# Layer 1 of a two-layer fp32 MLP: the third token tile's first products as seven block products, and another order of work at the layer boundary

## The chip, the cores and the metric

The kernel runs on one core of a Trainium2 chip. The metric is the device time of one execution in microseconds (us). The core has a matrix engine (PE, with its weight loads shown apart as PEld), a vector engine (DVE), an activation engine (ACT), a general engine (POOL) and a queue engine (SP) that issues the transfers; each takes its own instructions in order, and semaphores let one wait for another.

## The reference, cut to what matters

```python
# attention with a decay gives x: 1536 tokens x 512
h = x @ w_in;   g = h * tanh(softplus(h));   x = g @ w_out      # layer 1, d_ff = 2048
h = x @ w_in2;  g = h * sigmoid(h);          out = g @ w_out2   # layer 2
```

## The kernel before, in words

**Splitting.** A fp32 product is made of three products of a shorter type: each matrix is held as a high part (a cast, ACT) and a low part (what the cast lost, DVE or POOL), and a product is high x high, low x high and high x low, all added up in PSUM. A weight comes from memory as 512 KB by one transfer into a staging slot; ACT (L140, L141) and DVE (L172, L176) unpack it, ACT casts it (L240) and POOL makes its low part (L241). High and low parts live in places of an "arena" that are handed out by `take` and returned by `give`.

**Tiling.** There are three token tiles of 512 tokens (0, 1, 2), and the 2048 columns of a layer are taken in steps `p` of two slices of 128. Steps 0 to 7 are layer 1, steps 8 to 15 layer 2. The text below says "step 4" for p = 4.

**Seven instead of eight.** For tiles 0 and 1 together, the eight block products (two tiles, two halves of the inner dimension, two slices) are made as seven, by a scheme that multiplies sums of blocks: `m1, m5, m6, m2, m7, m3, m4`. Each is six matmuls of 128x512, so 42 for what would take 48. It needs sums of the token blocks (`sums`, made once per layer) and of the weight blocks (`T` for the first matrix, `S` for the second, `sum_pair`, on POOL). The same scheme serves the second products, `s1, s5, s6, s2, s7, s3, s4`. Tile 2 has no partner: its first products are `h0` and `h1` (12 matmuls of 128x512 each, L1160), its second ones `o0` and `o1` (12 each, L1215). From step 4 on, all of PSUM is eight banks Z0 to Z7 of 512 columns.

**What sets the order.** Nothing is scheduled by the compiler: the order on each engine is the order in which Python issues the instructions. For steps 4 to 15 (class `Step`) it is written out as a string per step in `plans`: visits parted by `;`, each a list of names. `m..`, `s..`, `h`, `o` are products with what follows them; `a0/a1` the activation of `h`, `l0/l1` its low part; `ts`, `n4` sums of activated blocks into the pad `F`; `q0/q1` their high and low parts; `p` begins unpacking a weight (ACT; a digit names the bank used as scratch), `d` is one unpacking or weight-summing operation (DVE or POOL), `w` puts one weight part into the arena. `into` adds a finished block into the layer's accumulators. At the end of each visit `pump` issues a transfer if a staging slot is free. Steps 2 and 3 (class `Block`, `m..` in the list `core`) and the second products of slices 4 to 7 (`emit_o`, list `os`) come just before step 4.

**Staging.** There are four slots: two of their own (`slot`) and two halves of `slab`. From step 8 on `slab` is an accumulator, so the last steps load through two slots only.

**The boundary.** Layer 2 needs all of layer 1's output: step 7 ends with the last additions, then the output is split again into high and low parts (`c00` ... `c11` for tiles 0 and 1, `x2` for tile 2), and the sums of blocks for layer 2 are made from it (`s_1`, `s_4`, `s_3`, then `hi`/`low`). Step 8 therefore uses eight plain products (`e0` to `e3`) in place of the seven; step 9 is the first that needs the sums.

Of the kernel before, what the change touches and what calls it, by code (L numbers as in the profile page):

```python
# [17 lines left out]
def decay_attention_mish_silu_kernel(  # L18
# [39 lines left out]
    slab = const.tile([P, 2048], F32, name="slab")  # L58
# [93 lines left out]
    made = {}  # L152
    adder = [nc.vector]
# [68 lines left out]
    def run_parts(k=None):  # L222
        for _ in range(len(parts) if k is None else min(k, len(parts))):
# [3 lines left out]
            homes_of[key] = take(True), take(True)  # L227
            hi, lo = [t.rearrange("p (k c) -> p k c", k=2) if len(key) > 2 else t for t in homes_of[key]]
            wtiles[key] = hi, lo
# [6 lines left out]
            else:  # L236
                uses_left[key] = 2
# [361 lines left out]
    def emit_o(t, n, first, last):  # L599
# [4 lines left out]
        if first:  # L604
            po[t] = [(ps_o, late[-1])[j // 2].tile([P, T], F32, tag="o", name="po") for j in range(4)]
# [83 lines left out]
    def make_sums(pool, other):  # L689
# [22 lines left out]
            [low(3, fx)],  # L712
        ])
# [166 lines left out]
    for i, (t, f) in enumerate(steps):  # L880
        n = i + PH
        if n == N:
# [7 lines left out]
            pads.append(late[0].tile([P, 4, T], F32, name="F"))  # L890
            eye = late[0].tile([P, P], F32, name="eye")
# [113 lines left out]
    for item in items:  # L1005
# [40 lines left out]
    class Step:  # L1046

        def __init__(self, p):
            self.p, self.mm = p, 2 * p // NF
            self.opens = p == NF // 2  # L1050
# [3 lines left out]
            self.Z = Z if self.mm == 0 else Z[6:] + Z[:6]  # L1054
            self.quad = [self.Z[2 * i : 2 * i + 2] for i in range(4)]

        def product(self, dst, xq, wq, start):
# [51 lines left out]
        def m4(self):  # L1109
            p = self.p  # L1110
            self.product(6, (1, 1), 3, False)
            for key in ((2 * p, 0), (2 * p + 1, 0), (p, "T", 0), (p, "T", 1)):
                read(key)
            self.split("21", self.Z[6])
# [31 lines left out]
        def part(self, k, low):  # L1146
# [5 lines left out]
            low.tensor_tensor(out=lo, in0=f, in1=hi.bitcast(F32), op=sub)  # L1152

# [42 lines left out]
        def q1(self):  # L1196
            self.part(1, nc.vector if self.late or self.opens else nc.gpsimd)
# [24 lines left out]
        def seed(self):  # L1222
            self.seeded = True
            self.po = [self.Z[i] for i in (2, 3, 6, 7)]
            for k in range(4):
                nc.scalar.copy(self.po[k], accs[self.mm, 2][:, k])

        def o0(self):
            if not self.po:
                self.po = [self.Z[i] for i in ((2, 3, 6, 7) if self.late else (0, 1, 4, 3) if self.opens else range(4))]  # L1230
# [59 lines left out]
        def s7(self):  # L1290
            self.second(0, 2, 1, False)
            self.into(0, 2, 0)
            if self.opens:
                accs[1, 1] = homes[0].tile([P, 4, T], F32, tag="acc", name="acc")
            self.into(1, 0, 3, True)

        def s3(self):
            self.second(2, 3, "22", False)
            self.into(0, 0, 2)
# [19 lines left out]
    def x2():  # L1319
        for k in range(4):  # L1320
            hi, lo = [x[:, k] for x in x_tile(2)]
            z = Z[(2, 3, 6, 7)[k]]
# [7 lines left out]
    def c(t, k, e):  # L1330
        cast_x(t, k)(e)

    def s_1():
        g = [F[:, 2:4], F[:, 0:2]]
        tt(out=g[0], in0=a1[:, 0:2], in1=a1[:, 2:4], op=add)
        lows[0] = cast(sums[0], g[0])
        tt(out=g[1], in0=g[0], in1=a0[:, 0:2], op=sub)
        lows[1] = cast(sums[1], g[1])
# [21 lines left out]
    def close(st):  # L1360
# [13 lines left out]
    extras = {"x2": x2, "s_1": s_1, "s_3": s_3, "s_4": s_4, "hi2": lambda: hi(2), "hi3": lambda: hi(3)}  # L1374
    extras |= {f"low{i}": lambda i=i: low(i) for i in range(4)}
    extras |= {f"c{t}{k}": lambda t=t, k=k: c(t, k, nc.gpsimd if k > t else nc.vector) for t in range(2) for k in range(2)}
    extras |= {"p": lambda: run_pre(1, 0), **{f"p{i}": lambda i=i: run_pre(1, 0, st.Z[i]) for i in (4, 5, 6, 7)}, "d": lambda: run_split(1, 0), "w": lambda: run_parts(1)}
    tail = "m7 d d; m3; m4 ts; h0 a0 q0 n4 w; l0 p6 h1 a1 q1 p4 w; d l1 d o0 d d; o1 w w d d; s1 d d; s5 w; s6; s2 w; s7; s3; s4 p4"
    steady = "m1 p5 d d; m5; m6 d d w w; m2 d d; " + tail
    plans = {  # L1380
        GF: "m1 p4 p5; m5; m6 d d d d; m2 w w d d; " + tail,
        NF // 2 - 1: "m1 p5 d d d d; m5; m6 w w; m2; m7; m3 ts; m4 n4 q0; h0 a0 l0; h1 a1 l1 q1; "
        "s1; s5 table w; s6 p w; s2; s7 c01 seed; s3 c00; s4 c11 c10; o0 s_1; o1",
        NF // 2: "e0 low0 low1 x2 d d; e1 s_4 p w; e2 s_3 d d; e3; h0 a0 w l0 d d d d ts; h1 a1 p l1 n4 q0 w q1 w d d; o0; o1 ; s1 p w; s5 d d; s6 d d d d w; s2; s7 hi2 w hi3 w; s3 low2; s4 p4",
        NF // 2 + 1: steady.replace("m6", "m6 low3"),
# [65 lines left out]
```

## Time and profile before

| | us |
|---|---|
| median of 3 runs | 551.08 (550.48 to 551.21) |
| the profiled execution | 551.02 |
| its span in the trace | 549.1 |
| PE busy | 539.3 (98%) |
| DVE / ACT / POOL busy | 404.0 / 338.2 / 288.3 |
| granted PE clock, mean | 0.999 |

The time is what the device took for the whole execution; the span runs from the first profiled instruction to the last, and 1.92 us of the time lie outside it. Matmuls are pipelined: a row shows 0.39 us for one of 128x512, though the next starts sooner. So the time that PE loses is read from starts: so many matmuls between two starts, at the spacing that a stretch without waits shows.

### The profile page before, as it was taken

Reading aid. Unit: us, or ns where it says so; the run is one execution under the profiler, and the core shown is the slowest. Engines: PE = TensorE matmul, PEld = TensorE weight load, DVE = VectorE, ACT = ScalarE, POOL = GpSimd, SP = SyncE. Lnnn points to the kernel's source line nnn. Section 1 sums busy time; section 2 is a strip of 40 time slices with the busy share of each in tenths; the row PEclk is TensorE's granted clock in tenths of the full one; section 3 lists DMA queues with packets and bytes.
Section 4 is the critical chain, followed back from the end, with each engine's and each line's share of the span. In section 5 each row is a group of like instructions: output and inputs, shape, how many; then the busy total and the mean of one; then the engine's idle time right before and its main releaser. Section 6 shows DMA issues by size and latency. Waiting matters only on the chain.

```text
span 549.1 us, 8856 instructions
## 1 busy us (share of the span) xinstructions
PE 539.3 (98%) x3306; PEld 438.7 (80%) x3306; DVE 404.0 (74%) x641; ACT 338.2 (62%) x620; POOL 288.3 (53%) x269
## 2 busy tenths in 40 slices
PE   9999999999999999999999999999999999999995
PEld 6878778888877788888878877888888888888875
DVE  5877956994485786786767987687778686867684
ACT  4788643863654747567666896666583847475631
POOL 4555630222034684948411485957576766849610
PEclk9999999999999999999999999999999999999999
DMA  8993450231012222222200022222211112222006
GB/s 301 391 329 134 130 181 1 77 116 38 17 60 76 78 76 78 77 78 77 78 0 2 0 77 78 76 78 76 66 63 66 50 66 77 78 76 76 2 0 230
DMA packets 14602, 49.85 MB, mean 91 GB/s; under 512 B 1632, under 2 KB 1888, under 8 KB 14560
## 3 DMA queue, kind: packets, MB, share of 16 engines
q1 hardware_dynamic: 14560, 49.29, 26.4%
q8 instruction: 26, 0.43, 0.3%
q14 instruction: 16, 0.13, 0.1%
HBM read 46.14 MB, written 3.15 MB: 90 GB/s over the span
## 4 chain that ended last, share of the span: by engine, by line
PE 79%; DVE 9%; ACT 5%; DMA 4%; issue 1%; SPq 1%; POOL 0%; DVEq 0%
PE z L1258 19%; PE z L1069 17%; PE z L1160 11%; PE z L1215 9%; PE ph L591 7%; PE po L619 6%; PE pu L640 5%; DMA xslot<-x 2%; DMA slab<-w 2%; PE b L736 1%; PE a L736 1%; DVE xl L1312 1%; DVE dec L176 1%; DVE arena L1152 1%; DVE dec L172 1%
## 5 line engine op out<-in xcount | busy, mean ns | idle before, releaser
L241 POOL TENSOR_TENSOR arena<-dec,arena 128x512 fp32r<-128x512 f32 x49 | 64.4, 1320 | 125.5 <-ACT arena L240 102.3
L1258 PE MATMUL z<-arena 128*128 128x512 f32 x376 | 96.0, 390 | 1.0 <-ACT slab L1280 1.0
L1258 PEld LDWEIGHTS z<-arena 128*128 128x128 f32 x376 | 70.3, 188 | 16.6 <-ACT slab L1280 1.4
L1152 POOL TENSOR_TENSOR arena<-F,arena 128x1024 fp32r<-128x1024 f32 x20 | 48.3, 2417 | 34.5 <-ACT arena L1151 34.5
L240 ACT CAST arena<-dec 128x512 fp32r<-128x512 f32 x56 | 35.0, 624 | 36.3 <-DVE dec L176 36.1
L241 POOL TENSOR_TENSOR arena<-t,arena 128x512 fp32r<-128x512 f32 x34 | 45.9, 1358 | 15.3 <-ACT arena L240 15.3
L1160 PE MATMUL z<-xh,arena 128*128 128x512 f32 x168 | 53.8, 389 | 0.0
L1215 PE MATMUL z<-arena 128*128 128x512 f32 x188 | 52.4, 390 | 0.0
L1282 DVE TENSOR_TENSOR acc<-z,acc 128x512 f32<-128x512 f32 x76 | 47.7, 681 | 4.8 <-PE z L1258 4.8
L1069 PE MATMUL z<-xh,arena 128*128 128x512 f32 x182 | 50.1, 391 | 0.6 <-DVE z L1101 0.5
L1282 DVE TENSOR_TENSOR slab<-z,slab 128x512 f32<-128x512 f32 x60 | 38.6, 683 | 10.3 <-PE z L1258 10.2
L240 ACT CAST arena<-t 128x512 fp32r<-128x512 f32 x38 | 23.6, 622 | 35.6 <-POOL t L209 29.9
L1215 PEld LDWEIGHTS z<-arena 128*128 128x128 f32 x188 | 35.2, 188 | 7.7 <-DVE F L1142 0.4
L1069 PEld LDWEIGHTS z<-xh,arena 128*128 128x128 f32 x182 | 33.9, 188 | 8.7 <-DVE z L1101 1.3
L591 PE MATMUL ph<-xh,arena 128*128 128x512 f32 x124 | 39.3, 394 | 0.4 <-ACT arena L240 0.4
L1160 PEld LDWEIGHTS z<-xh,arena 128*128 128x128 f32 x168 | 31.5, 188 | 6.6
L172 DVE SCALAR_TENSOR_TENSOR z<-z,slot 128x512 uint32<-128x512 uint32 x34 | 23.5, 692 | 16.4 <-ACT slot L141 16.2
L1160 PE MATMUL z<-xl,arena 128*128 128x512 f32 x88 | 34.2, 389 | 0.0
L640 PE MATMUL pu<-arena 128*128 128x512 f32 x132 | 33.8, 400 | 0.2 <-ACT arena L240 0.2
L140 ACT ACTIVATE z<-slot 128x512 f32<-128x512 f32 x34 | 21.7, 638 | 17.9 <-DVE slab L1282 11.9
L209 POOL TENSOR_TENSOR t<-dec 128x256 f32<-128x256 f32 x42 | 31.2, 742 | 0.0
L619 PE MATMUL po<-arena 128*128 128x512 f32 x128 | 30.7, 393 | 0.1
(263 smaller groups left out, 1279.1 us busy)
## 6 DMA issues: line engine op xcount, KB each, us to landing
slot<-w SPq DMA_DIRECT2D x46, 512.0 KB, 3.7
xslot<-x SPq DMA_DIRECT2D x24, 512.0 KB, 7.2
slab<-w SPq DMA_DIRECT2D x18, 512.0 KB, 3.8
out<-F SPq DMA_DIRECT2D x8, 256.0 KB, 2.1
out<-acc SPq DMA_DIRECT2D x3, 256.0 KB, 2.7
out<-acc SPq DMA_DIRECT2D x2, 128.0 KB, 2.5
factors<-lam SPq DMA_DIRECT2D x1, 0.0 KB
```

What stands on the lines that cost most here:

```text
L209: adder[0].tensor_tensor(out=t[:, k], in0=in0, in1=in1, op=op)
L240: nc.scalar.copy(hi, f)
L241: nc.gpsimd.tensor_tensor(out=lo, in0=f, in1=hi.bitcast(F32), op=ALU.subtract)
L591: nc.tensor.matmul(ph, lhsT=wi[wsel][:, kk * P : (kk + 1) * P], rhs=xt[xsel][:, kk, :], start=(i == 0), stop=(i == 3 * KD - 1),)
L619: nc.tensor.matmul(po[t][j][:, c], lhsT=lhsT, rhs=rhs, start=(first and wsel + gsel == 0), stop=(last and gsel == 1 and c.stop == T),)
L640: nc.tensor.matmul(banks[j], lhsT=wtiles[f, 1][ws][:, js[j] * P : js[j] * P + P], rhs=gts[f, t][gs], start=(i < 2), stop=(i >= len(passes) ...
L1069: nc.tensor.matmul(self.Z[dst], lhsT=w[ws][:, kk * P : (kk + 1) * P], rhs=x[xx][:, kk, :], start=(start and i == 0), stop=True, skip_group ...
L1152: low.tensor_tensor(out=lo, in0=f, in1=hi.bitcast(F32), op=sub)
L1160: nc.tensor.matmul(z, lhsT=w[ws][:, kk * P : (kk + 1) * P], rhs=x[xx][:, kk, :], start=(i == 0), stop=True, skip_group_check=True,)
L1215: nc.tensor.matmul(banks[k], lhsT=lhsT, rhs=rhs, start=(j == 0 and ws + gs == 0 and not self.seeded), stop=True, skip_group_check=True,)
L1258: nc.tensor.matmul(self.quad[dst][k], lhsT=w[ws][:, k * P : (k + 1) * P], rhs=g[gs], start=(start and i == 0), stop=True, skip_group_check ...
L1282: tt(out=to, in0=self.quad[src][k], in1=to, op=add)
```

## The change: seven block products over two token halves

The token tile 2 is cut into two halves of 256 tokens, which take the places of tiles 0 and 1 in the scheme. In steps 4 to 7 (`paired`), `u1, u5, u6, u2, u7, u3, u4` replace `h0, h1`: seven block products of six matmuls of 128x256. They use the weight sums `T` that are there already, and token sums made once by `half_sums` (14 additions of 128x512 on DVE, four casts on ACT), run one entry per visit among steps 2 and 3. Two of the eight sums live in the arena for good, the others in the `slab`, which is therefore no staging slot from the weights of slices 8 on; steps 4 to 8 load through two slots, as steps 9 to 15 did. The first half of an odd slice's weight is then needed in no product of its own, so its cast and its low part are made for 256 columns (L240, L241).

The other edits: the second products of tile 1 in `emit_o` get four other banks than those of tile 0; the order in steps 4 to 9 is written anew; in step 7 the `s` products come ahead of `o0, o1`; `q1` of step 9 makes its low part on DVE; `s_1`, `s_4`, `s_3` go to step 8's `h1` visit; the banks of layer 2 are numbered otherwise.

```diff
+            if t == 1 and n // GF == 1:
+                po[t] = [bank("po") for j in range(4)]
...
+        def half(self, dst, xq, wq, start):
...
+            order = [(ws, xx, kk) for ws, xx in ((0, 0), (1, 0), (0, 1)) for kk in range(2)]
+            for i, (ws, xx, kk) in enumerate(order):
+                nc.tensor.matmul(
+                    self.Y[dst], lhsT=w[ws][:, kk * P : (kk + 1) * P], rhs=x[xx][:, kk, :],
+                    start=(start and i == 0), stop=True, skip_group_check=True,
+                )
+        def u1(self):
+            self.Y = [self.Z[4 + i % 3 % 2][:, 256 * s : 256 * s + 256] for i, s in ((0, 0), (1, 1), (1, 0), (0, 1))]
+            self.half(0, (0, 0), (0, 0), True)
+            nc.scalar.copy(self.Y[1], self.Y[0])
+        def u5(self):
+            self.half(3, 0, 0, False)
+            nc.scalar.copy(fifth, self.Y[3])
+        def u6(self):
+            self.half(1, 1, 1, False)
+            tt(out=self.Y[2], in0=self.Y[1], in1=fifth, op=add)
...
+        def b(self, k):
...
+            for j, y, c in self.halves(k):
+                nc.scalar.activation(self.g2[j][0][:, c], y, self.fn)
+            nc.scalar.activation(self.Z[4 + k], self.Z[4 + k], self.fn)
...
-            (kept if n // 2 == NF // 2 and i else slots).append(held.pop((n, i)))
+            (kept if n // 2 == GF - 1 and i else slots).append(held.pop((n, i)))
...
-        GF: "m1 p4 p5; m5; m6 d d d d; m2 w w d d; " + tail,
+        **{p: both for p in paired},
+        GF: both.replace("u1; m1 p0", "m1; u1 p0"),
...
-        NF // 2: "e0 low0 low1 x2 d d; e1 s_4 p w; e2 s_3 d d; e3; h0 a0 w l0 d d d d ts; h1 a1 p l1 n4 q0 w q1 w d d; o0; o1 ; s1 p w; s5 d d; s6 d d d d w; s2; s7 hi2 w hi3 w; s3 low2; s4 p4",
-        NF // 2 + 1: steady.replace("m6", "m6 low3"),
+        NF // 2: "e0 x2 w; e1 d d; e2 p d d w; e3 d d; h0 a0 ts n4; h1 l0 w q0 a1 l1 q1 w s_1 s_4 s_3; o0 p; o1 d d; s1; s5 hi0 low0 d d; s6 ; s2 d d w; s7 w p; s3 hi1 low1; s4",
+        NF // 2 + 1: "m1 hi2 low2 p0; h0 a0 hi3 w d d w; h1 d d l0 a1; m5 w; m6 low3 l1; m2 d d w; m7 d d; m3; m4 ts p3; q0 n4 o0 w d d; o1 q1 p2 d d; s1 w d d; s5 w d d; s6 w; s2 w; s7; s3; s4 p4",
```

On PE, the start of step 4. Before: m1, m5, m6, m2, m7 follow each other (`z_2025` is Z2, `z_2026` Z3, `z_2029` Z6; `xh`/`xl` are token tiles, `sh`/`sl` their sums, `arena`/`more` weights).

```order
L1069 MATMUL z_2025<-xh,arena 128x512 x4
L1069 MATMUL z_2025<-xl,arena 128x512 x2
L1069 MATMUL z_2026<-sh,more 128x512 x2
L1069 MATMUL z_2026<-sh,arena 128x512 x2
L1069 MATMUL z_2026<-sl,more 128x512 x2
L1069 MATMUL z_2029<-sh,more 128x512 x2
L1069 MATMUL z_2029<-sh,arena 128x512 x2
L1069 MATMUL z_2029<-sl,more 128x512 x2
L1069 MATMUL z_2025<-xh,arena 128x512 x4
L1069 MATMUL z_2025<-xl,arena 128x512 x2
L1069 MATMUL z_2029<-sh,arena 128x512 x2
```

The same place now, from m6 to m7 (`z_2050` is Z6, `z_2049` Z5, `z_2048` Z4, `z_2046` Z2; `halves` are the sums of the token halves).

```order
L1126 MATMUL z_2050<-sh,arena 128x512 x2
L1126 MATMUL z_2050<-sh,more 128x512 x2
L1126 MATMUL z_2050<-sl,arena 128x512 x2
L1191 MATMUL z_2049<-halves,arena 128x256 x2
L1191 MATMUL z_2049<-halves,more 128x256 x2
L1191 MATMUL z_2049<-halves,arena 128x256 x2
L1191 MATMUL z_2048<-xh,arena 128x256 x4
L1191 MATMUL z_2048<-xl,arena 128x256 x2
L1126 MATMUL z_2046<-xh,arena 128x512 x4
L1126 MATMUL z_2046<-xl,arena 128x512 x2
L1191 MATMUL z_2049<-arena 128x256 x6
L1126 MATMUL z_2050<-sh,arena 128x512 x4
```

Between the two products that add into Z6 stand u6, u2, m2 and u7 in place of m2 alone.

On DVE, the layer boundary. Before, the sums for layer 2 stand at the end of step 7 and in step 8's first visits (`F<-acc` is the first of `s_1`; the four `xl<-z` rows are `x2`; `acc<-acc,F` is `s_4`, `acc<-acc` `s_3`).

```order
L1335 TENSOR_TENSOR F<-acc 128x1024
L1337 TENSOR_TENSOR F<-F,acc 128x1024
L1312 TENSOR_TENSOR sl<-F,sh 128x1024 x2
L1324 TENSOR_TENSOR xl<-z_2025,xh 128x512
L1324 TENSOR_TENSOR xl<-z_2026,xh 128x512
L1324 TENSOR_TENSOR xl<-z_2029,xh 128x512
L1324 TENSOR_TENSOR xl<-z_2030,xh 128x512
L172 SCALAR_TENSOR_TENSOR dec<-dec,slab 128x512
L176 SCALAR_TENSOR_TENSOR dec<-slab,dec 128x512
L1344 TENSOR_TENSOR acc<-acc,F 128x1024
L1081 TENSOR_TENSOR arena<-z_2023,arena 128x512
L1341 TENSOR_TENSOR acc<-acc 128x1024
```

Now the same sums stand behind step 8's last low parts (`L1330` is `l1`, `L1285` `q1`), ahead of the unpacking of slice 19 and of `low0`.

```order
L1330 TENSOR_TENSOR arena<-z_2047,arena 128x512
L1285 TENSOR_TENSOR arena<-F,arena 128x1024
L1505 TENSOR_TENSOR F<-acc 128x1024
L1506 TENSOR_TENSOR F<-F,acc 128x1024
L1512 TENSOR_TENSOR acc<-acc,F 128x1024
L1509 TENSOR_TENSOR acc<-acc 128x1024
L174 SCALAR_TENSOR_TENSOR dec<-dec,slot_80 128x512
L178 SCALAR_TENSOR_TENSOR dec<-slot_80,dec 128x512
L1481 TENSOR_TENSOR sl<-F,sh 128x1024
L1446 TENSOR_TENSOR acc<-z_2044,acc 128x512
L1446 TENSOR_TENSOR acc<-z_2045,acc 128x512
```

The four additions of 128x1024 have left the stretch between step 7's last products and step 8's `h0`, and stand beside `o0`, `o1` and the `s` products of step 8.

## Rows read from the trace of the kernel before

**Rows 1.** The page's first part: busy us (share of the span) and instructions of each engine.

```profile
PE 539.3 (98%) x3306; PEld 438.7 (80%) x3306; DVE 404.0 (74%) x641; ACT 338.2 (62%) x620; POOL 288.3 (53%) x269
```

**Rows 2.** The chain of waits, in order of time: start us, us, what.

```profile
213.97 5.44 PE z L1160 x24
...
224.88 9.52 PE z L1258 x42
...
264.35 9.69 PE z L1069 x42
...
297.61 1.15 DVE F L1335
```

**Rows 3.** Timeline of PE, tile 1's second products to step 4's `m4`: start us, us, instruction, [idle before].

```profile
160.68 3.47 PE L619 MATMUL po<-arena 128*128 128x512 f32 x11
163.99 1.09 PE L619 MATMUL po<-more,arena 128*128 128x512 f32 x4
...
172.19 1.07 PE L619 MATMUL po<-more,arena 128*128 128x512 f32 x4
173.36 1.19 PE L1069 MATMUL z<-xh,arena 128*128 128x512 f32 x4
...
182.35 0.74 PE L1069 MATMUL z<-xh,arena 128*128 128x512 f32 x2 [0.24 <-DVE z L1101]
...
183.86 0.39 PE L1160 MATMUL z<-xh,arena 128*128 128x512 f32 x1
```

**Rows 4.** Timeline of PE at the layer boundary, steps 7 to 9.

```profile
279.31 1.52 PE L1258 MATMUL z<-arena 128*128 128x512 f32 x6
...
289.39 0.63 PE L1215 MATMUL z<-arena 128*128 128x512 f32 x2
...
311.18 3.40 PE L1215 MATMUL z<-arena 128*128 128x512 f32 x13
...
316.91 0.39 PE L1258 MATMUL z<-arena 128*128 128x512 f32 x1
...
327.93 0.61 PE L1069 MATMUL z<-xh,more 128*128 128x512 f32 x2
...
338.82 0.39 PE L1160 MATMUL z<-xh,more 128*128 128x512 f32 x1
```

**Rows 5.** Timeline of PE and of its weight loads at the kernel's last matmuls.

```profile
542.52 0.28 PE L1366 MATMUL z<-arena,more 128*128 128x256 f32 x1
...
543.00 0.28 PE L1366 MATMUL z<-more,arena 128*128 128x256 f32 x1
...
542.88 0.19 PEld L1366 LDWEIGHTS z<-more,arena 128*128 128x128 f32 x1
```

**Rows 6.** Busy time by stretch: window, length, then PE, PEld, DVE, ACT, POOL (instructions), clock.

```profile
131.00:172.00 41.00, 40.90 (x179) 32.94 (x178) 25.04 (x36) 19.97 (x36) 10.85 (x8) 1.00 0.16 52
...
184.00:274.00 90.00, 90.00 (x398) 74.24 (x397) 66.90 (x107) 56.95 (x99) 61.40 (x54) 1.00 0.23 76
```

**Rows 7.** Groups of instructions, shapes apart: busy us, mean ns of one, idle before.

```profile
L1101 DVE TENSOR_TENSOR z<-z,F 128x512 f32<-128x512 f32 x11 | 7.7, 698 | 7.4 <-PE z L1069 7.4
L672 DVE TENSOR_TENSOR fx<-fx,xl 128x1024 f32<-128x1024 f32 x4 | 4.9, 1224 | 0.0
L538 DVE TENSOR_TENSOR xl<-px,xh 128x256 fp32r<-128x256 f32 x8 | 3.4, 419 | 7.5 <-ACT xh L533 7.5
...
L533 ACT CAST xh<-px 128x256 fp32r<-128x256 f32 x8 | 2.9, 367 | 1.6 <-PE px L409 1.5
L1311 ACT CAST sh<-F 128x1024 fp32r<-128x1024 f32 x2 | 2.1, 1053 | 2.9 <-DVE F L1335 2.6 <-DVE F L1337 0.3
```

**Rows 8.** Timelines of DVE and ACT in step 8's `s` products.

```profile
316.81 2.31 DVE L1152 TENSOR_TENSOR arena<-F,arena 128x1024 fp32r<-128x1024 f32 x1
...
322.11 2.04 ACT L1280 COPY slab<-z 128x512 f32<-128x512 f32 x4
```

**Rows 9.** The page's part on transfers: out<-in, count, KB each, us to landing.

```profile
slot<-w SPq DMA_DIRECT2D x46, 512.0 KB, 3.7
```

More of the change, by code (lines that the diff above doesn't have):

```diff
@@ L152, in decay_attention_mish_silu_kernel @@
     made = {}
+    paired = range(GF, NF // 2)
     adder = [nc.vector]
@@ L226, in run_parts @@
             f, key = parts.pop(0)
-            homes_of[key] = take(True), take(True)
-            hi, lo = [t.rearrange("p (k c) -> p k c", k=2) if len(key) > 2 else t for t in homes_of[key]]
-            wtiles[key] = hi, lo
+            if len(key) < 3 and not key[1] and key[0] % 2 and key[0] // 2 in paired:
+                homes_of[key] = (take(True),)
+                hi, lo = [homes_of[key][0][:, 256 * j : 256 * j + 256] for j in range(2)]
+                f = f[:, 256:]
+                wtiles[key] = hi, lo
+            else:
+                homes_of[key] = take(True), take(True)
+                hi, lo = [t.rearrange("p (k c) -> p k c", k=2) if len(key) > 2 else t for t in homes_of[key]]
+                wtiles[key] = hi, lo
             if len(key) > 2:
@@ L236, in run_parts @@
             else:
-                uses_left[key] = 2
+                uses_left[key] = 2 - (key[0] // 2 in paired and not key[1])
             ready.add(key)
@@ L604, in emit_o @@
         if first:
-            po[t] = [(ps_o, late[-1])[j // 2].tile([P, T], F32, tag="o", name="po") for j in range(4)]
+            if t == 1 and n // GF == 1:
+                po[t] = [bank("po") for j in range(4)]
+            else:
+                po[t] = [(ps_o, late[-1])[j // 2].tile([P, T], F32, tag="o", name="po") for j in range(4)]
         passes = [(j, wsel, gsel) for j in range(4) for wsel, gsel in ((0, 0), (1, 0), (0, 1))]
@@ new lines, in u7, with u3, u4, halves @@
+        def u7(self):
+            self.half(1, 2, 2, False)
+            tt(out=self.Y[3], in0=self.Y[1], in1=fifth, op=add)
+        def u3(self):
+            self.half(2, 3, (1, 1), False)
+        def u4(self):
+            self.half(1, (1, 1), 3, False)
+        def halves(self, k):
+            return [(j, self.Y[y], slice(256 * (y % 2), 256 * (y % 2) + 256)) for j, y in (((0, 0), (1, 3)), ((0, 1), (1, 2)))[k]]
+        def b(self, k):
+            if not self.g2:
+                self.g2 = {j: (take(), take()) for j in range(2)}
+            for j, y, c in self.halves(k):
+                nc.scalar.activation(self.g2[j][0][:, c], y, self.fn)
+            nc.scalar.activation(self.Z[4 + k], self.Z[4 + k], self.fn)
@@ L1196, in q1 @@
         def q1(self):
-            self.part(1, nc.vector if self.late or self.opens else nc.gpsimd)
+            self.part(1, nc.vector if self.late or self.opens or self.next else nc.gpsimd)
         def l1(self):
@@ L1291, in s7 @@
             self.second(0, 2, 1, False)
+            if self.early and self.late:
+                self.into(1, 0, 3)
             self.into(0, 2, 0)
@@ L1294, in s7 @@
                 accs[1, 1] = homes[0].tile([P, 4, T], F32, tag="acc", name="acc")
-            self.into(1, 0, 3, True)
+            if not self.early:
+                self.into(1, 0, 3, True)
         def s3(self):
             self.second(2, 3, "22", False)
+            if self.early and not self.late:
+                self.into(1, 0, 3)
             self.into(0, 0, 2)
```

147 lines of the change are left out of this document (123 added, 24 removed).

## The prediction, made blind

> **What bounds the kernel now.** I read the page's busy times first: PE is busy 98% of the span, every other engine 74% or less [rows 1]. So the end is set by how many matmuls there are and by the moments in which PE waits, and other engines matter only where PE waits for them. The chain of waits agrees: most of it is PE. It also gives the price of a matmul that waits for nothing: 42 of 128x512 in 9.52 us, 24 in 5.44 us, both 0.2267 us each [rows 2]. From there I went through PE's timeline and compared starts with counts; whatever exceeds 0.2267 us each is lost.
>
> Two stretches that the change touches lose time; between and behind them, nothing (row 224.88 is one of many equal ones).
>
> *Around the start of step 4*: 11 matmuls from 160.68 to 163.99 take 3.31 instead of 2.49 us, 0.82 lost; four from 172.19 to 173.36 take 1.17 instead of 0.91, 0.26 lost; step 4's 42 block products take from 173.36 to 183.86, 10.50 instead of 9.52, 0.98 lost [rows 3]. Sum 2.06.
>
> *At the layer boundary*: step 7's block products 9.69 instead of 9.52, 0.17 lost [rows 2]; its `s` products 279.31 to 289.39, 10.08 instead of 9.52, 0.56; step 8's `o` products 311.18 to 316.91, 5.73 instead of 5.44, 0.29; its `s` products 316.91 to 327.93, 11.02 instead of 9.52, 1.50; step 9's block products 327.93 to 338.82, 10.89 instead of 9.52, 1.37 [rows 4]. Sum 3.89.
>
> **The change part by part.**
>
> *Fewer columns on PE.* Each of steps 4 to 7 drops 24 matmuls of 128x512, 24 x 0.2267 = 5.44 us, and gets 42 of 128x256. The trace has few of that size: four intervals from 542.52 to 543.00, 0.120 us each, with a new weight every time [rows 5]. 42 x 0.120 = 5.04 us. Saved 0.40 us a step, 1.60 us in four. The bounds: 0.1133, half of the long matmul, would save 2.7 us in all; 0.1295 (5.44 / 42) would save nothing. I take 0.120, which is the shape itself. The Trainium skill, page "TensorE: Matmul & The Clock Gate", section "Back-to-back issue gap", lists 262 cycles for 256 columns and 518 for 512, 0.109 and 0.216 us at 2.4 GHz; by it a step would save 0.59 us, four 2.4 us, and the sum below would end 0.8 us lower. The rows show 0.2267 and 0.120, so the page's figures are short here.
>
> *Waits around step 4.* The 0.82 us are tile 1's second products waiting for DVE to empty the banks that tile 0 just used (four additions). They now go to banks 4, 1, 5 and 0, which the blocks of step 3 have left by then: gone. The 0.26 us before step 4 are its `m1` waiting for one of the same banks, Z2, which is now free: gone; `u1`, which does take bank 4, comes 1.36 us later, behind an addition of about 0.70 [rows 7]. Inside step 4 `m7` and `m4` add into Z6, and must wait until DVE has read it (`Z7 = Z6 + F`, `Z3 = Z6 + F`; the last wait is marked DVE L1101 [rows 3]). Only m2, 1.36 us, stood between m6 and m7; now u6, u2, m2 and u7 do, 3 x 0.72 + 1.36 = 3.5 us, and u3, u4 and m3 between m7 and m4, 2.8 us. An addition needs 0.70 us [rows 7], and one unpacking of a weight (two DVE operations, 1.3 us) may stand ahead of it: covered. All 2.06 us go; the same cover removes step 7's 0.17.
>
> *What pays for it off PE.* Per paired step: two copies and four activations of 256 columns (0.37 us each if like the nearest row, [rows 7]) replace two activations of 512; DVE gets two additions and four low parts of 256 (0.42 each, [rows 7]) for two of 512, about 1.1 us more; the half-width part saves 0.3 us on ACT and 0.65 us on POOL. DVE is busy 66.90 of 90 us in these steps [rows 6]: room. On the path within a step: the activations behind u4 (two of 256, one of 512, some 1.2 us) and the low parts behind them (0.8 us) must end before the third matmul of o0; m3, m4 and two matmuls, 2.72 + 0.45 us, cover them with 1 us to spare. The blocks' sums (`ts`, `q0`, `q1`) lose h0 and h1 as cover, but `o0`, `o1` and `s1` (6.8 us) still stand ahead of s5, the first to need them: about 5.7 us behind m4's end for the last low part on POOL, against 8.2 us until s6. Thinnest is the step's end: `into` behind s3 must empty Z2 before the next m1, by my count with 0.5 us left.
>
> *The sums of token halves.* 14 additions of 512 elements (half of 1224 ns, 0.61 us, [rows 7]), 8.6 us, and four casts, fall between 127 and 150 us, where DVE is idle 16 of 41 us and POOL nearly so [rows 6]. The block additions that PE waits for there start at the moment their product ends even with one sum ahead of each: nothing on the path.
>
> *Staging.* With two slots from slice 8 on, SP's loads wait for the unpacking of the slot (L176) instead of running ahead. A load lands 3.7 us after its issue [rows 9], and by the plans a slot is asked for again five products or more behind the visit that frees it, 6.8 us; steps 9 to 15 do so today and PE loses nothing in them. Cost nothing; if a load came late, ACT would stand at L140 with all behind it.
>
> *The layer boundary.* Step 7: s1 to s4 ahead of o0, o1 means that tiles 0 and 1 are complete 5.44 us earlier, so that their splitting (four casts of 1.05 us, four low parts of 1.22 us, [rows 7]) runs under o0 and o1 in place of s-products and e-products. That takes `q1` off DVE (the 0.56 us) and, with `s_1`, `s_4`, `s_3` moved to step 8's h1, frees DVE before `h0`; before, DVE is the chain itself from 297.61 us on [rows 2]. Step 9 gets h0 and h1 between m1 and m5, 5.44 us for POOL's T parts and DVE's low parts, on which m5 to m4 waited (1.37 us). Following my rows for ACT and DVE through the new order, I find every product of steps 7 to 9 ready except one: s7 of step 8. ACT has behind o1's end four copies, two copies (s1), two copies (s5), the cast `hi0` and one copy, about 9 x 0.52 + 1.05 = 5.7 us ([rows 7, 8]: 2.04 us for four copies), and s7 wants to start 4 x 1.36 = 5.44 us behind it: 0.3 us, and 0.1 for PE to start again. DVE's run in the same place (q1, three sums and `s_3`, one unpacking, `low0`: 6 x 1.22 + 1.3 = 8.7 us) has 1.6 us of slack, and a 1024-wide low part beside POOL took 2.31 us in place of 1.23 [rows 8]: I add 0.2 us. New waits 0.6 us, between 0 and 1.2.
>
> **Sum**, against the profiled execution's 551.02 us (0.06 us under the median): 551.02 - 1.60 - 2.06 - 3.89 + 0.60 = 544.07.
>
> **The rivals.**
>
> *The boundary makes new waits.* The DVE run of step 8 holds five operations with both inputs in SBUF; POOL's parts fall beside it. One contested operation costs 1.1 us [rows 8]; from the second on, s4 waits for `into` and step 9's `low2`, l0 and Z7 come late in turn. At two to four us of new waits the time is 546 to 548. For it: the same engine made the chain here before. Against: each step's slack is over 0.5 us by my count.
>
> *The short matmul is bound by its weight load.* A load's row is 0.19 us [rows 5]. If loads could not overlap each other, 42 would take 7.9 us, 2.46 more than the 24 they replace, 9.8 in four steps: 551.02 + 9.8 - 5.95 + 0.6 = 555.5, slower than before. It decides from 0.161 us a matmul on: there the extra 168 x 0.032 eats the 5.35 us. Against it: loads of 0.19 us already start 0.12 us apart in rows 5. The Trainium skill, same page, section "Part 3: Packing small matmuls", says that a load runs under a matmul only in other row groups; with full-height weights it would then add to each matmul, and more, shorter matmuls would lose. The trace disagrees: with loads of 0.19 us added, matmuls could not start every 0.2267 us [rows 2] or every 0.120 us [rows 5], each with a new full weight.
>
> *Only the columns go.* Each wait moves to the next thing that is late, and nothing but 1.60 us is saved: 549.4.
>
> *The sums of halves hold up step 2 and 3.* Were each as slow as a contested one, 14 x 1.7 = 24 us in 16 idle ones, PE would end 8 us later, near 552. POOL's 10.9 us there [rows 6] lie behind 149 us.
>
> **How the numbers follow.** Forecast 0.56, new waits at the boundary 0.28, only the columns 0.06, load-bound 0.05, sums of halves 0.03, something else 0.02. Predicted: 544.1. The forecast's own range is 543.2 (no new wait, 0.118 us a matmul) to 545.2; with most of the second case the range goes to 547.5. About 0.2%, 1.1 us, is what a measurement can tell from no change. Faster: 0.56 + 0.28 + 0.05 of the third; slower: load-bound, and a share of the last two.
>
> **What would show it.** Right: in the changed trace 42 matmuls of 128x256 in 5.04 us; tile 1's second products and step 4's `m1` start without a wait; steps 5 to 7 last 29.5 instead of 29.9 us; from step 4 to step 9 PE loses under 1.2 us, most of it before s7 of step 8. Wrong: spacing over 0.13 us; PE waiting for DVE in step 8's s4 or step 9's m7 and m4; ACT standing at L140 for a transfer; PE waiting among the blocks of steps 2 and 3.

## The result and the profile after

| | before | after |
|---|---|---|
| median, us | 551.14 (550.48 to 551.41, 4 runs) | 545.64 (545.26 to 545.73, 4 runs) |
| the profiled execution, us | 551.02 | 545.26 |
| its span, us | 549.1 | 543.5 |

The ratio is 0.9901, with a 95% interval of 0.9884 to 0.9918: faster, and clear of the 0.2% that the prediction calls no change. The page's first part, which answers to [rows 1] (busy us, share of the span, instructions):

```profile
PE 535.2 (98%) x3378; PEld 441.3 (81%) x3378; DVE 419.5 (77%) x672; ACT 342.0 (63%) x642; POOL 284.1 (52%) x270
```

PE still bounds the kernel, with 4.1 us less of busy time; DVE has 15.5 us more. Where the time went is read from the starts of PE's products. The first three rows are of PE's timeline before (the start of the second products of slices 4 to 7, of step 8 and of step 10), the next four of after (the start of the second products and of steps 4, 8 and 10); columns: start us, us, instruction.

```profile
155.92 1.29 PE L619 MATMUL po<-arena 128*128 128x512 f32 x5
...
294.86 1.07 PE L1069 MATMUL z<-xh,arena 128*128 128x512 f32 x4
...
359.22 1.07 PE L1069 MATMUL z<-xh,arena 128*128 128x512 f32 x4
```

```profile
155.44 5.60 PE L630 MATMUL po<-arena 128*128 128x512 f32 x24
...
171.76 1.07 PE L1126 MATMUL z<-xh,arena 128*128 128x512 f32 x4
...
290.34 0.84 PE L1126 MATMUL z<-xh,arena 128*128 128x512 f32 x3
...
353.62 1.07 PE L1126 MATMUL z<-xh,arena 128*128 128x512 f32 x4
```

With step 4's start before, 173.36 [rows 3], that gives a sheet that closes:

| stretch | before | after | difference | forecast |
|---|---|---|---|---|
| to the second products of slices 4 to 7 | 155.92 | 155.44 | -0.48 | 0 |
| these 72 products | 17.44 | 16.32 | -1.12 | -1.08 |
| steps 4 to 7 | 121.50 | 118.58 | -2.92 | -3.31 |
| steps 8 and 9 | 64.36 | 63.28 | -1.08 | -2.56 |
| step 10 to the span's end | 189.88 | 189.88 | 0 | 0 |
| outside the span | 1.92 | 1.76 | -0.16 | 0 |
| sum | 551.02 | 545.26 | -5.76 | -6.95 |

(The forecast's -3.31 is -1.60 for columns and -0.98, -0.17, -0.56 for waits; its -2.56 is -0.29, -1.50, -1.37 and +0.60.) The change moved 5.12 us; the first line and the one outside the span are not its doing, as e11 shows below. Two lines fell short: steps 4 to 7 by 0.39 us, steps 8 and 9 by 1.48.

**Steps 4 to 7.** The chain of waits, in order of time (start us, us, what), for step 5's first products:

```profile
201.56 0.71 PE z L1191 x6
202.27 2.75 PE z L1126 x12
205.02 0.71 PE z L1191 x6
205.73 1.39 PE z L1126 x6
207.12 1.43 PE z L1191 x12
```

Six short matmuls take 0.71 us, twelve 1.43: 0.119 each, as forecast. But the six or twelve long ones behind them take 1.39 and 2.75 us where 1.36 and 2.72 were due. In the trace the first five long matmuls behind short ones start 0.232 us apart on average, the ones after them 0.2267 again. The 20 such places in four steps cost 0.5 us. The same intervals stand behind waits too: in the kernel before, the long matmuls behind the wait at 173.36 [rows 3] and its restart start 0.231, 0.235, 0.229, 0.232 and 0.231 us apart, then 0.227; in step 5 now, behind six short ones, it is 0.233, 0.236, 0.228, 0.232, 0.231, then 0.227. So they are not a mark of short matmuls alone. Every wait that the prediction saw in steps 4 to 7 is gone.

**Steps 8 and 9.** PE's timeline in step 9's s6 and s7; in brackets the idle time and who ended it:

```profile
345.23 0.63 PE L1422 MATMUL z<-arena 128*128 128x512 f32 x2
346.18 1.65 PE L1422 MATMUL z<-arena 128*128 128x512 f32 x6 [0.32 <-DVE arena L1285]
...
348.35 0.39 PE L1422 MATMUL z<-more,arena 128*128 128x512 f32 x1
349.37 0.50 PE L1422 MATMUL z<-arena,more 128*128 128x512 f32 x1 [0.64 <-DVE acc L1446]
349.71 0.39 PE L1422 MATMUL z<-arena 128*128 128x512 f32 x1
```

Two matmuls from 345.23 to 346.18 take 0.95 us instead of 0.45, and the restart adds 0.11 (the second matmul behind a wait starts some 0.335 us after the first, not 0.227): 0.60 lost in step 9's s6, which waits for the low part of q1. One from 348.35 to 349.37 takes 1.02 instead of 0.23, and again 0.11: 0.90 lost in s7, which waits for a bank that `into` has to read. Step 9's m4 loses 0.29, step 8's s7 0.15 to 0.17. Together that is 1.95 us; by their lengths against 270 matmuls at 9.52/42 us the two steps lose 2.08, against 3.16 before. DVE's timeline in the same stretch:

```profile
342.51 2.48 DVE L1408 TENSOR_TENSOR acc<-z,acc 128x512 f32<-128x512 f32 x4
344.91 1.21 DVE L1285 TENSOR_TENSOR arena<-F,arena 128x1024 fp32r<-128x1024 f32 x1
346.04 0.69 DVE L174 SCALAR_TENSOR_TENSOR z<-z,slot 128x512 uint32<-128x512 uint32 x1
346.83 0.69 DVE L178 SCALAR_TENSOR_TENSOR dec<-slot,z 128x512 uint32<-128x512 uint32 x1
347.44 2.48 DVE L1446 TENSOR_TENSOR acc<-z,acc 128x512 f32<-128x512 f32 x4
```

From the end of o1 on DVE has no pause: o1's four additions, q1, the unpacking of a weight, then the additions behind s5 and s6. The third of these, which frees s7's bank, ends at 349.31, 6.8 us after 342.51; PE makes s1, s5, s6 and s2 meanwhile, 24 x 0.2267 = 5.44 us. The chain of waits says the same from its side: it leaves PE at 320.6 us and comes back at 349.37.

```profile
312.26 8.35 PE z L1422 x36
...
333.23 1.68 POOL t L211
...
335.75 0.62 ACT arena L248
336.38 0.50 ACT arena L1134
...
344.99 1.13 DVE arena L1285
...
348.63 0.69 DVE acc L1446
...
349.37 4.41 PE z L1422 x18
```

Read upwards: s7 waited for DVE, DVE had started its run late because ACT stood at a cast (L248) until POOL had made a weight sum, with two activations queued behind that cast. (In the part left out, the chain has 5.46 us from 323.91 on as POOL's issue; POOL's timeline says that it waited there for another cast of ACT.) Two rows of DVE's and ACT's timelines show that step 9 has contested work as well:

```profile
332.19 2.12 DVE L1481 TENSOR_TENSOR xl<-acc,xh 128x1024 fp32r<-128x1024 f32 x1
...
335.75 0.62 ACT L248 CAST arena<-t 128x512 fp32r<-128x512 f32 x1 [1.79 <-POOL t L211]
```

The first is low3, 2.12 us beside POOL where such a low part alone takes 1.22. It stands ahead of the addition that m4 waits for. POOL's sum beside it took 1.72 us, the next one 0.73.

### The profile page after: what moved, and what is told of

It reads as the page before. It is cut to its first block, busy times and chain, and to the rows that moved or that the text cites. A ratio compares the mean times of both kernels' runs of the same rounds, so it can differ in the third digit from the quotient of the medians.

```text
span 543.5 us, 9063 instructions
## 1 busy us (share of the span) xinstructions
PE 535.2 (98%) x3378; PEld 441.3 (81%) x3378; DVE 419.5 (77%) x672; ACT 342.0 (63%) x642; POOL 284.1 (52%) x270
## 4 chain that ended last, share of the span: by engine, by line
PE 86%; DVE 3%; DMA 3%; issue 2%; ACT 2%; POOL 2%; SPq 1%; DVEq 0%; POOLq 0%
PE z L1422 20%; PE z L1126 20%; PE z L1373 11%; PE ph L599 7%; PE z L1318 7%; PE po L630 6%; PE pu L651 5%; PE z L1191 4%; DMA xslot<-x 2%; PE b L778 2%; POOL arena L249 1%; PE a L778 1%; SPq L311 1%; PE px L407 1%; PE px L417 1%
## 5 line engine op out<-in xcount | busy, mean ns | idle before, releaser
L249 POOL TENSOR_TENSOR arena<-dec,arena 128x512 fp32r<-128x512 f32 (+1 forms) x55 | 70.9, 1291 | 108.3 <-ACT arena L248 95.1
L1422 PE MATMUL z<-arena 128*128 128x512 f32 x374 | 102.2, 390 | 0.4 <-DVE arena L1285 0.3
L1446 DVE TENSOR_TENSOR acc<-z,acc 128x512 f32<-128x512 f32 x136 | 85.1, 682 | 8.3 <-PE z L1422 8.2
L248 ACT CAST arena<-dec 128x512 fp32r<-128x512 f32 (+1 forms) x58 | 35.5, 611 | 34.4 <-DVE dec L178 34.4
L1373 PE MATMUL z<-arena 128*128 128x512 f32 x220 | 57.0, 389 | 0.0
L248 ACT CAST arena<-t 128x512 fp32r<-128x512 f32 x46 | 28.2, 620 | 44.7 <-POOL t L211 37.3
L1126 PE MATMUL z<-xh,arena 128*128 128x512 f32 x192 | 52.1, 391 | 0.0
L1126 PEld LDWEIGHTS z<-xh,arena 128*128 128x128 f32 x192 | 35.4, 188 | 7.3 <-DVE z L1158 0.4
L1285 POOL TENSOR_TENSOR more<-F,arena 128x1024 fp32r<-128x1024 f32 x10 | 24.2, 2418 | 30.3 <-ACT arena L1284 20.1
L1318 PE MATMUL z<-xh,arena 128*128 128x512 f32 x120 | 37.7, 389 | 0.0
L142 ACT ACTIVATE slot<-slot 128x512 uint32<-128x512 uint32 x56 | 37.3, 666 | 0.0
L1126 PE MATMUL z<-sh,arena 128*128 128x512 f32 x114 | 31.5, 391 | 0.0
L178 DVE SCALAR_TENSOR_TENSOR dec<-slot,z 128x512 uint32<-128x512 uint32 x41 | 28.2, 687 | 3.5
```

The costliest lines, as they stand in the source:

```text
L248: nc.scalar.copy(hi, f)
L249: nc.gpsimd.tensor_tensor(out=lo, in0=f, in1=hi.bitcast(F32), op=ALU.subtract)
L1126: nc.tensor.matmul(self.Z[dst], lhsT=w[ws][:, kk * P : (kk + 1) * P], rhs=x[xx][:, kk, :], start=(start and i == 0), stop=True, skip_group ...
L1318: nc.tensor.matmul(z, lhsT=w[ws][:, kk * P : (kk + 1) * P], rhs=x[xx][:, kk, :], start=(i == 0), stop=True, skip_group_check=True,)
L1373: nc.tensor.matmul(banks[k], lhsT=lhsT, rhs=rhs, start=(j == 0 and ws + gs == 0 and not self.seeded), stop=True, skip_group_check=True,)
L1422: nc.tensor.matmul(self.quad[dst][k], lhsT=w[ws][:, k * P : (k + 1) * P], rhs=g[gs], start=(start and i == 0), stop=True, skip_group_check ...
```

## The experiments

Times are medians. Beside them stand stretches of the traces, which repeat to 0.05 us where neither they nor the order ahead of them was changed. The kernel before gave 551.21 us beside e1 to e4, 551.02 beside e5 to e8, 550.87 beside e9 to e11 and 551.24 beside e12.

### The banks of tile 1's second products: e1 and e2

e1 makes the first edit of the change, four other banks (`bank("po")`) for tile 1, in the kernel before and nothing else.

> The kernel before, with the one edit that gives tile 1's second products of slices 4 to 7 four other banks. Theory of the prediction: the 0.82 us among these products and the 0.26 us before step 4's m1 are waits for banks that tile 0's results have not left yet, so the edit alone gives about 1.1 us: 550.0, and the 0.98 us inside step 4 stay. Rival: step 4 of the kernel before uses banks 4 and 5 at once as scratch for two weights, and ACT then stands behind DVE's additions, so that the wait only moves: 550.8 or more.

549.46 us, ratio 0.9967 (0.9955 to 0.9980). PE's timeline of e1, from these products to step 4's m4:

```profile
171.98 1.07 PE L1072 MATMUL z<-xh,arena 128*128 128x512 f32 x4
...
180.84 0.73 PE L1072 MATMUL z<-xh,arena 128*128 128x512 f32 x2 [0.25 <-DVE z L1104]
```

The 72 products take 16.32 us instead of 17.44, with no wait, and the wait inside step 4 (180.84) stands as it did in [rows 3]. e2 takes the edit out of the changed kernel.

> The changed kernel with that edit undone: tile 1's second products use tile 0's banks again. Theory: 0.8 to 1.1 us come back, 546.4 to 546.8, as short waits among the second products that start near 155 us. Rival: the changed order around step 4 hides them, 545.6.

547.42 us. The same rows in e2:

```profile
156.32 5.60 PE L627 MATMUL po<-arena 128*128 128x512 f32 x24
...
173.78 1.21 PE L1123 MATMUL z<-xh,arena 128*128 128x512 f32 x4
```

Now 72 products last 17.46 us: 1.14 us are back, and 0.15 in step 4, mostly a restart. So the edit is worth 1.1 us among these products and 1.3 us with what follows, in either kernel. The times moved by 1.75 and 1.78, in e2 0.6 us beyond what was expected. The traces account for 1.36 and 1.29 of that from the first of these products to the last matmul; the rest is of the size by which one kernel's starts differ from run to run (e11).

### What the columns are worth: e3, e10, e5

```diff
-            self.half(3, 0, 0, False)
...
-            self.half(1, 1, 1, False)
...
-            self.half(1, 2, 2, False)
...
-                    self.Y[dst], lhsT=w[ws][:, kk * P : (kk + 1) * P], rhs=x[xx][:, kk, :],
+                    y, lhsT=w[ws][:, kk * P : (kk + 1) * P], rhs=x[xx][:, kk, :],
```

In e3, `y` is a whole bank and `x` all 512 columns.

> The changed kernel, but u1, u2, u3 and u4 multiply all 512 columns and u5, u6 and u7 make no product: 24 matmuls of 128x512 a step as before the change, everything else in the new order (so the third tile's results of steps 4 to 7 are not those of the reference). By the sum on record (0.120 against 0.2267 us, 5.04 against 5.44 us a step) it takes 1.6 us longer: 547.2. By the changed trace, in which the first long matmuls behind short ones start some 0.03 us late in all, five times a step, the columns give only 1.1 us: 546.7. Rival: the short products also bring waits or hide some, and it takes under 0.5 us or over 2.5 us longer.

550.69 us, 5.0 more: the rival's over 2.5 us, but no measure of the columns, since u2 now writes all of the bank that u5's copy reads, so PE waits for ACT once in each of steps 4 to 6. In step 4:

```profile
178.69 1.21 PE L1190 MATMUL z<-xh,arena 128*128 128x512 f32 x4 [0.69 <-ACT fifth L1201]
```

With a wait of 0.33 us in step 7 these make 3.6 of the 5 us. e10 moves the copy and u7's addition to the other bank.

> As e3 (u1, u2, u3, u4 at 512 columns, no products in u5, u6, u7; the third tile's results are not the reference's), but what u5 and u7 copy and add lies in the other bank, so that u2 waits for nothing. Theory: the columns alone are worth 4 x 0.40 = 1.6 us less the late starts behind short matmuls, 0.5 us in four steps, so 1.1 us longer than the changed kernel: 546.7, and 119.7 us from step 4's to step 8's start instead of 118.58. By the sum on record: 547.2 and 120.2.

547.54 us, against 546.39 for the changed kernel beside it (e11). Steps 4 to 7 last 120.03 instead of 118.58 us. Of the 1.45, 0.33 is the wait that is left in step 7 (the chain runs through ACT and DVE there); 1.12 us are the columns, less the late starts behind the short ones. The chain of e10 in step 5 has no late start:

```profile
202.67 1.36 PE z L1190 x6
204.03 4.08 PE z L1126 x18
```

> The changed kernel with every matmul of u1 to u7 issued twice, so 84 instead of 42 of 128x256 a step in steps 4 to 7, 168 more in all (the third tile's results are then not the reference's). Theory: a short matmul with a new weight costs 0.120 us in any run of them, so 168 x 0.120 = 20.2 us more: 565.8. Rival: runs of 12 and more are held to the weight loads' 0.19 us, and only runs of six are carried by loads made ahead: 168 x 0.19 = 31.9 us more, 577.5.

```diff
-            for i, (ws, xx, kk) in enumerate(order):
+            for i, (ws, xx, kk) in enumerate(order + order):
```

Steps 4 to 7 last 138.64 us, 20.06 more for 168 matmuls: 0.119 each in runs of 12 and 24 too, and not one PE wait there. The load-bound rival is out. The time, 568.75, is 23.1 us above the changed kernel's and 3 above what was expected; what the steps do not explain lies in the start (1.75 us in the profiled run) and the end, where the eight output transfers took 4.3 us each instead of 2.2. Why they did stays open.

### What makes the waits in step 9: e7, e4, e8, e9, e12

> The changed kernel with the low part of step 9's q1 back on POOL, where it stood before the change. Theory A (the queue of DVE as a whole makes the waits in step 9's s products): POOL takes 2.4 us from 344.7 us on, s6 waits for it some 1.5 us instead of 0.6, and s7, which waited 0.9 for DVE, waits for nothing: 545.6 within 0.3, the wait only changes its place. Theory B (moving q1 to DVE made the waits): both go, 544.1.

```diff
-            self.part(1, nc.vector if self.late or self.opens or self.next else nc.gpsimd)
+            self.part(1, nc.vector if self.late or self.opens else nc.gpsimd)
```

545.75 us. PE's timeline of e7 in s6, and POOL's:

```profile
347.56 1.67 PE L1422 MATMUL z<-arena 128*128 128x512 f32 x6 [1.20 <-POOL arena L1285]
```

```profile
345.13 2.38 POOL L1285 TENSOR_TENSOR arena<-F,arena 128x1024 fp32r<-128x1024 f32 x1
```

s6 loses 1.48 us in place of 0.60, s7 nothing in place of 0.90: theory A to the point. Putting q1 on DVE in step 9 was worth nothing, and did not cost anything either: off DVE it is as late on POOL.

e4 unpacks one weight earlier, shares q1 and moves l1. The plan of step 9, only the visits that differ, before and after the edit:

```diff
- m6 low3 l1; m2 d d w; m7 d d; m3; m4 ts p3; ... o1 q1 p2 d d;
+ m6 low3; m2 p0 d d w; m7 l1 d d; m3; m4 d d ts p3; ... o1 q1;
```

> The changed kernel with another order in step 9: a weight is unpacked on DVE in an idle 1.3 us beside m4 and no longer between q1 and the additions behind s5; q1's low part is made half on DVE, half on POOL; l1 stands behind m7's addition. Theory: DVE's queue from o1's end to s7 (6.8 us of work in a row for 5.4 us of products) makes the 1.50 us of waits in step 9's s6 and s7, and l1 the 0.29 us before m4; all go, 545.6 - 1.8 = 543.8. Rival: something else is as late (POOL's weight parts for step 10, the transfers), and the waits move to step 10's first products: 545.0 or more.

545.84 us: no gain that a time could show. From step 8's start to the last matmul the trace has 246.57 us instead of 247.03: m4's wait is gone, but s6 now loses 1.24 us, and s7 nothing. DVE's timeline, then POOL's:

```profile
346.08 1.52 DVE L1359 TENSOR_TENSOR arena<-F,arena 128x512 fp32r<-128x512 f32 x1
```

```profile
345.77 1.28 POOL L1359 TENSOR_TENSOR arena<-F,arena 128x512 fp32r<-128x512 f32 x1
```

Half of q1 took DVE 1.52 us, more than the whole had taken alone (1.21). Both halves read two inputs from SBUF at the same time. Besides, l1 and the unpacking had made DVE's run into o1 0.4 us later. e8 parts the two halves in time and puts l1 into another gap:

```diff
- m5 w; m6 low3 l1; m2 d d w; ... m4 ts p3; ... o1 q1 p2 d d; s1 w d d; s5 w d d; s6 w; s2 w;
+ m5 l1 w; m6 low3; m2 p0 d d w; ... m4 d d ts p3; ... o1 q1; s1 w q3 d d; s5 W; s6 w d d; s2 w;
```

(`q1` makes its first half on DVE, `q3` the second on POOL; `W` takes the second weight part in the line.)

> The changed kernel with another order in step 9, of which only places differ from e4: one weight is unpacked in DVE's idle 1.3 us beside m4 and the other beside o0, l1 stands in DVE's idle 0.9 us ahead of m5's addition, q1's low part is half on DVE (needed by s6) and half on POOL later, at a time when DVE makes no two-operand work from SBUF, and of step 10's weight parts the first sum goes ahead. Theory: DVE's run from o1's end to s7's banks is then 2.7 + 0.6 + 1.4 + 0.7 = 5.4 us, as long as the products it runs beside, so s6, s7 and m4 start without a wait: 545.6 - 1.8 = 543.8, and in the trace the time from step 8's start to the last matmul falls from 247.03 to 245.3 us. Rival: POOL and DVE collide on the way, as in e4, where half of q1 took 1.52 us beside POOL's half: 245.3 is missed by 0.5 us or more.

547.46 us, 1.8 slower than the changed kernel. The profiled execution is the longest of the six (546.80 to 549.42), so what follows stands for the upper end; what the others lost, no trace shows. Step 9 did most of what was expected: steps 8 and 9 last 61.82 us instead of 63.28. But step 10 lost 4.1 us. PE's timeline of e8, ACT's, then the busy times of one stretch (window, length, PE, PEld, DVE, ACT, POOL, granted clock, share and GB/s of DMA):

```profile
358.41 1.72 PE L1126 MATMUL z<-sh,arena 128*128 128x512 f32 x4 [2.27 <-ACT z L1142]
359.93 1.05 PE L1126 MATMUL z<-sl,arena 128*128 128x512 f32 x2
360.78 1.77 PE L1126 MATMUL z<-xh,arena 128*128 128x512 f32 x4
```

```profile
356.14 0.62 ACT L248 CAST arena<-t 128x512 fp32r<-128x512 f32 x1 [3.53 <-POOL t L211]
...
357.77 0.58 ACT L1142 COPY z<-z 128x512 f32<-128x512 f32 x1
```

```profile
359.20:362.40 3.20, 3.20 (x10) 2.48 (x9) 1.50 (x3) 1.30 (x3) 1.28 (x1) 0.52 0.49 146
```

ACT stood 3.53 us at a cast for POOL's late sum, and the copy that m6 needs (L1142) was queued behind it. PE waited; and after the wait its granted clock was 0.52 of full speed in this stretch, the lower of its two levels, 1.2 GHz: two matmuls from 359.93 to 360.78, 0.425 us each instead of 0.2267. So a wait of 2.4 us cost some 1.6 us more. e9 puts POOL's order back and makes q1's second half on DVE behind s6's additions (`s6 q3 w`).

> As e8, but the weight parts of step 10 stand in the order of the changed kernel, and the second half of q1's low part is made on DVE behind the additions of s6, not on POOL. Theory: e8's new wait of 2.4 us before step 10's m6 comes from ACT standing at a cast for POOL's late weight sum, with the copy that m6 waits for behind it; with POOL 1.3 us freer and the old order it goes, and the gains in step 9 (1.46 us in e8's trace) stay: from step 8's start to the last matmul 245.4 us instead of 247.03, time 544.1. Rival: POOL is late for step 10 even so, since the products now come 1.5 us earlier: over 246 us and 544.8.

544.84 us, beside 546.39 for the changed kernel; steps 8 and 9 61.77 us, step 10 without the new wait, 245.90 us from step 8's start to the last matmul. The half of q1 is now 0.68 us:

```profile
345.34 0.68 DVE L1358 TENSOR_TENSOR arena<-F,arena 128x512 fp32r<-128x512 f32 x1
```

That missed the expected 245.4 by 0.5 us; the time is the rival's 544.8, and 245.90 lies just under its 246. Steps 8 and 9 gave the 1.5 us, though s6 still lost 0.36; 0.37 us went in small pieces over steps 10 to 15 (184.12 us from step 10's start to the last matmul instead of 183.75), and why is not known. The last experiment takes the cast at which the chain of the changed kernel had turned from POOL to ACT:

```diff
- m2 p0 d d w; m7 d d; m3;
+ m2 p0 d d; m7 d d; m3 w;
```

> As e9, and the cast of the first weight sum of slices 18 and 19 stands behind the copy of m3's block on ACT and no longer ahead of the two activations before it. Theory, from the changed kernel's chain of waits: ACT stands at this cast until POOL's sum (1.72 us beside DVE's 2.12 us low3) is done, and with it the activation behind it and DVE's run into o1 and s6; in e9 that still costs s6 0.36 us. With the cast behind them, that wait goes: 245.90 - 0.35 = 245.55 us from step 8's start to the last matmul, 544.5. Rival: DVE's unpacking beside m4 is as late as ACT, and s6 waits 0.3 us as in e9.

544.35 us, ratio to the kernel before 0.9873 (0.9857 to 0.9890). PE's timeline from s1's start to step 10's:

```profile
342.84 1.98 PE L1431 MATMUL z<-arena 128*128 128x512 f32 x8
...
352.36 1.07 PE L1126 MATMUL z<-xh,arena 128*128 128x512 f32 x4
```

42 products from 342.84 to 352.36, 9.52 us: no wait left in step 9. From step 8's start to the last matmul 245.34 us, 1.69 less than in the changed kernel. This version is faster than both kernels: the changed kernel's ratio is 0.9901, and 0.9913 (0.9900 to 0.9927) in e11. From step 10's start on it takes 0.2 us more than the changed kernel, as e9 did.

### The place of the four additions: e6

```diff
- e0 x2 w; e1 d d; e2 p d d w; ... h1 l0 w q0 a1 l1 q1 w s_1 s_4 s_3;
+ e0 s_1 x2 w; e1 s_4 d d; e2 s_3 p d d w; ... h1 l0 w q0 a1 l1 q1 w;
```

> The changed kernel with the four additions of 128x1024 (s_1, s_4, s_3) back ahead of step 8's h0, in its visits e0, e1 and e2, about where they stood before the change. Theory of the prediction: 4.9 us of DVE work then hold up the low parts and the F sums of step 8, and part of the 1.80 us that its o and s products lost before the change comes back: 546.4 to 547.4. Rival: with step 7's s products ahead of o0 and o1 DVE is free early enough, and the place of the four additions is worth nothing: 545.6.

552.85 us, 7.2 slower, far beyond the expected 0.8 to 1.8. (The sums in F are overwritten by step 8's `ts` before the casts read them, so layer 2 gets other sums than the reference's; the work is the same.) From step 8's start to the last matmul it takes 253.35 us instead of 247.03. Two rows of DVE's timeline (s_1's second addition and l0), then PE's, then the busy times and granted clock of a stretch:

```profile
299.13 2.13 DVE L1506 TENSOR_TENSOR F<-F,acc 128x1024 f32<-128x1024 f32 x1
...
313.20 0.67 DVE L1330 TENSOR_TENSOR arena<-z,arena 128x512 fp32r<-128x512 f32 x1
```

```profile
313.93 6.42 PE L1373 MATMUL z<-arena 128*128 128x512 f32 x20 [4.18 <-DVE arena L1330]
```

```profile
314.60:317.50 2.90, 2.90 (x9) 2.28 (x8) 2.90 (x4) 1.57 (x3) 1.28 (x1) 0.52 0.03 6
```

The four additions, 1.22 us each when alone, take 6.6 us beside POOL's weight parts (1.22, 2.13, 1.57, 1.71). PE loses 0.8 us ahead of h0; then l0 comes 4.2 us late for o0, and the granted clock stands at the lower level, 0.52, for some nine matmuls, 0.2 us lost on each. Step 8 takes 38.31 us instead of 31.45, step 9 gets 0.6 back. In the kernel before the same additions stood at about this place and all of step 8 lost 1.79 us, so e6 shows what their place is worth in the new order, not what moving them gained over the old one.

### The changed kernel once more: e11

> The changed kernel itself, beside the two others on one chip: 545.6, with 247.0 us from step 8's start to the last matmul. What differs from run to run should lie ahead of 131 us.

546.39 us, 0.75 above its first runs. Its row for the second products, to be held against 155.44:

```profile
156.57 0.62 PE L630 MATMUL po<-arena 128*128 128x512 f32 x2
```

The same kernel came there 1.13 us later; from there on every stretch is as long as in the first trace (16.32, 118.59, 247.00). In all 14 traces the matmul that the changed kernel starts at 131.17 starts between there and 132.92, and from it to the second products it is 24.25 to 24.27 us, before the change as after it. So up to a microsecond between two medians, and the first line of the sheet above, are the start's, which the change does not touch.

## Why the prediction was right, and where it was not

It said 544.1 in a range of 543.2 to 547.5, and 545.64 lies in it, above the forecast's own part (to 545.2) and just under the rival's (546 to 548).

- **Waits around step 4, -2.06: right**, and for its reason. The 1.08 us at the banks measured 1.12 by the trace and 1.1 by e1 and e2; the 0.98 in m7 and m4 and step 7's 0.17 and 0.56 are gone. That the products put between them cover the first two fits the traces (in e1, without them, the waits stand); no run parts step 7's 0.56 from the rest of the new order.
- **Columns, -1.60: the price of a short matmul was right** (0.119 for 0.120), **the saving was not**: 1.12 by e10. The rows at hand showed short matmuls behind short ones only; what a long one behind them costs no row of before showed, and the sum put it at nothing. It was 0.5 us in four steps. (The trace of before has the same intervals behind waits.) The estimate by the figures of the Trainium skill ("TensorE: Matmul & The Clock Gate", "Back-to-back issue gap"), 2.4 us, is further off still.
- **Staging, the sums of halves, the work off PE, at no cost: right.** PE loses nothing from 131 us to step 4 nor, but for the late starts, in steps 4 to 7; no engine stands at a transfer there.
- **Boundary waits, -3.89, and new ones, +0.60: the term that was mis-sized.** Steps 8 and 9 lose 2.08 us instead of 0.60. Step 8's s7 is late, as said, by 0.15 where 0.4 was forecast. The other 1.8 us are in step 9's m4, s6 and s7, which the prediction found ready. It shows prices for DVE's queue in step 8's run of eight operations, but none for the same kind of run in step 9, where the plan writes `o1 q1 p2 d d`: some 2.5 + 1.2 + 1.4 us ahead of the additions that s7 waits for. The rows to price it were there. How much of the old 3.16 us each edit of the order removed, no run parts.
- **The first rival** named the mechanism (contested operations, `into` late on DVE) and a price of 2 to 4 us, but step 8's s4 as the place. What came true is its lower edge in the next step: low3 and POOL's sum were contested, m4 waited for DVE, and `into` was late for s7, though behind a run in which nothing was contested (q1 took 1.21 us). In waits this rival came nearer than the forecast, which had twice its chance. A third of the error, 0.64 of 1.83 us, is hidden in the profiled time by what the start and the time outside the span gave. That was luck for the number, though not for the range: 545.26 and 0.64 are 545.9, and e11 gave 546.39.
- **Load-bound: refuted** (e5). **Only the columns go: refuted** (e1, and the sheet). **Sums of halves late: refuted** by the trace.
- **What would show it**: two signs held (the short spacing, no wait at the second products and m1). Steps 5 to 7 last 29.65 us each, between the 29.5 forecast and the 29.9 before. The bound of 1.2 us of waits from step 4 to step 9 did not hold, nor was most of it before s7 of step 8 (0.17 of 2.08); and one sign of being wrong came true, PE waiting for DVE in step 9's m4, 0.29 us.

## What to carry to other kernels

When an order is rewritten, add up each engine's queue between two events of the bound engine, for every stretch that the new order touches: 6.8 us of work beside 5.4 us of products is a wait, whatever single operation it is booked to, and moving one operation to another engine (e7) only moves the wait. Before such a move, look at who else reads two inputs from SBUF at that time, and at what is queued behind a cast that waits for another engine. A saving in columns is to be priced with its neighbours: where wide and narrow matmuls alternated here, the wide ones behind narrow ones paid.

## What the hardware showed

- Behind a wait, the second matmul of 128x512 starts 0.31 to 0.34 us after the first instead of 0.227, mostly 0.335: some 0.11 us on top of each wait read here.
- PE's granted clock fell to the lower level (0.52 in the stretches read) behind waits of 2.3 us (e8) and 4.2 us (e6), for some ten matmuls; behind all waits of 1.2 us or less in the other kernels it did not. The Trainium skill, "TensorE: Matmul & The Clock Gate", "Part 1: The HAM clock gate", says that an idle PE falls to 1.2 GHz and that activity brings 2.4 back; the rows agree: 0.425 us a matmul in the stretch behind e8's wait, 0.2267 later.
- A two-input operation of DVE from SBUF is stretched while POOL does the same: 0.68 to 1.52 us for 128x512 (e9, e4), 1.22 to 2.13 for 128x1024 (e6). Operations with one input in PSUM stayed at 0.68 beside the same POOL work. The Trainium skill, "SBUF — State Buffer", "Who interferes with whom", says that only the port pair of these two engines contends, and that it is locked, not shared. The trace agrees on who contends, and comes near to a lock: in e4 POOL's half ends at 347.05 and DVE's at 347.60, 0.55 us behind it, where 0.68 is what it takes alone.
- Why the long matmuls behind short ones start late stays open. e10 shows that it goes with the short ones; the same intervals behind PE's waits say that it comes without short ones too.
